# Sums of exponentials in four column tiles throughout, and the last sums one round later

## The chip, the cores and the metric

The kernel runs on one core of a Trainium2 chip. A core has five engines that work side by side, each from its own queue in order: TensorE (PE; matrix products into PSUM, with the weight loads counted apart as PEld), VectorE (DVE), ScalarE (ACT), GpSimd (POOL) and SyncE (SP, which here issues nearly all DMA transfers). The metric is the device time of one execution in microseconds, the median over several runs; lower is better. A profiled execution gives a trace, and from it a page and the answers of views.

## The reference

Attention over 4 batches and 8 heads, 768 positions, 64 dimensions each. Queries and keys are assigned to one of 16 clusters by the largest cosine with that head's centroids, and a query sees only keys of its own cluster. Then a feed-forward block (FFN) with a squared ReLU over all 3072 rows.

```
mask = q_assign[:, :, :, None] == k_assign[:, :, None, :]
scores = scale * np.matmul(q, k.transpose(0, 1, 3, 2))
scores = np.where(mask, scores, -1000000000.0)
...
attn = np.exp(scores)
attn = attn / (np.sum(attn, axis=-1, keepdims=True) + 1e-09)
x = np.matmul(attn, v)      # (B,H,S,D) -> (B*S, H*D)
r = np.maximum(x @ w_in, 0.0)     # 512 -> 2048
out = (r * r) @ w_out             # 2048 -> 512
```

The diff touches `np.sum(attn)` and the division by it.

## The kernel before

**Tiling.** Heads go in pairs: pair 0 to 15, four to a batch, the two heads of a pair (`e` = 0, 1) on 64 partitions each. A pair has two halves `h` of 384 queries (`TB`), and a half takes six chunks of 128 keys, two to a step. The steps are the list `units` (line 725), 96 of them: first the first halves of pairs 0 to 3 (units 0 to 11), then their second halves (12 to 23), then pairs 4 to 15 with both halves each (24 to 95).

**One unit.** `scores` (line 439) multiplies queries and keys on TensorE and takes the exponential on ScalarE. For pairs 0 to 3 the mask goes into the same products, for the others VectorE applies it (line 470). `times_v` (line 502) multiplies the exponentials with v into the PSUM tile `av`, 64 rows for each head.

**The sums.** They are products with a constant block `ups`, so each row of the result holds the same sum. For the first halves of pairs 0 to 3 they are taken from the exponentials by 8 products for each unit, in the tile `sm` of the same pool as `av` (`ps_av`, two buffers). For all other halves GpSimd adds the exponentials of a half up in `acc` (lines 480 and 482), and `add_up` (line 529) forms the sums from `acc` with four products when the half is complete. Each fp32 product is two matmul instructions in the trace.

`ones_products` (line 486) has two forms. The usual one splits the 384 queries into two groups, so that two heads by two groups fill four column tiles of 32 rows, each over 192 columns. The `wide` form, for pair 3's first half alone (line 498), uses two column tiles of 64 rows, each over all 384 columns, so that every row of `av` finds its sum on its own partition.

**The division.** In the usual form `add_up` takes the reciprocal `r` of 192 columns (line 551), writes one row of each tile to memory (`far_r`, line 554), reads it back spread over 64 partitions for each head (`rb`, line 558), and puts a copy in `seen` (line 555), which is checked at the end for sums that are too small (`check_sums`, line 866). In between, `seen` is issued ahead of `rb` on SP. In a first half `av` is copied to `xT` by ScalarE before (line 536). One round later `finish` (line 567) multiplies by `rb`. In the wide form the reciprocal of 384 columns goes straight to `rb` (line 545), and `finish` follows in the same round, from `av`.

**The order.** The main loop (line 791) runs a round for each unit: its scores; `ends(added)`, the `finish` of halves that `add_up` has handled in the round before; the `times_v` of earlier units (one round behind, and from unit 12 on in twos, in the odd rounds); `add_up` of completed halves (for second halves of pairs 0 to 3 one round later, through the list `late`); rounding of the FFN's weights on ScalarE, VectorE and GpSimd (line 141; lines 150 to 166; up to round 23); and `fill_steps`.

`fill_steps` (line 746) issues plain FFN products of batch 0 between the attention's work (the generator `ffn`, line 579: for each half 64 products `ph` of 384 columns and 48 products `po` of 512). The share of a round is worked out from the columns left, less a reserve of three `po` products; from round 13 on it is given in even rounds only, for two at a time. A half's FFN becomes available when `finish` of pair 3 has been issued for it: for the first half in round 12. After the loop the rest is issued, and then batches 1 to 3 go through `ffn_pair` (line 610), seven block products in place of eight, with eight PSUM banks, till the end.

This is the order of the source; the framework's planner works out each engine's queue from it, by priority (`high_priority` raises it) among the instructions that its own estimate holds to be ready, and sets the waits.

Of the kernel before, what the change touches and what calls it, by code (L numbers as in the profile page):

```python
# [8 lines left out]
F32 = mybir.dt.float32  # L9
# [9 lines left out]
P = 128  # L19
# [6 lines left out]
def kernel(  # L26
# [10 lines left out]
    nc = tc.nc  # L37

    B, H, S, D = q.shape
    C = centroids.shape[1]  # L40
    NCH = S // P
# [4 lines left out]
    HP = H // 2  # L46
    NB = NCH // 2
    TB = NB * P
# [382 lines left out]
    sums = {}  # L431
# [4 lines left out]
    av = {}  # L436
# [46 lines left out]
                out=acc[pair, h], in0=acc[pair, h], in1=t[:, 2 * i : 2 * i + 2], op=ALU.add  # L483
            )

    def ones_products(sm, wide, e, rhs, first, last):

        n = TB if wide else TB // 2
        rows = P * n // (2 * TB)
        return [  # L490
            dict(
                out=sm[rows * r : rows * (r + 1)], lhsT=ups[:, 0:rows],
                rhs=rhs[:, n * i : n * (i + 1)], start=first, stop=last,
            )
            for i, r in enumerate(range(e * P // (2 * rows), (e + 1) * P // (2 * rows)))
        ]

    def wide(pair, h):

        return (pair, h) == (HP - 1, 0)  # L500

    def times_v(pair, h, c):
        if c == 0:
            av[pair, h] = ps_av.tile([P, TB], F32, name="av", tag="av")
            if first_half(pair, h):
                n = TB if wide(pair, h) else TB // 2
                sums[pair, h] = ps_av.tile([P, n], F32, name="sm", tag="av")
        t = ex.pop((pair, h, c))
        products = [
            dict(  # L510
                out=av[pair, h][D * e : D * (e + 1)], lhsT=raw_v[pair][:, e, c + i],
                rhs=t[:, 2 * i + e], start=(c + i == 0), stop=(c + i == NCH - 1),
            )
            for i in range(2) for e in range(2)
        ]
        if first_half(pair, h):
            for i in range(2):
                one = [
                    ones_products(
                        sums[pair, h], wide(pair, h), e, t[:, 2 * i + e], c + i == 0, c + i == NCH - 1  # L520
                    )
                    for e in range(2)
                ]
                products += [p for both in zip(*one) for p in both]
        together(products, 4000)
# [3 lines left out]
    def add_up(pair, h):  # L529


        b, hp = divmod(pair, HP)
        if first_half(pair, h):
            sm = sums.pop((pair, h))
            if not wide(pair, h):
                nc.scalar.copy(out=xT_of(b, h)[:, hp], in_=av.pop((pair, h)))
        else:
            total = acc.pop((pair, h))
            sm = bank("sm", [P, TB // 2])
            one = [ones_products(sm, False, e, total[:, e], True, True) for e in range(2)]  # L540
            together([p for both in zip(*one) for p in both])
        row = 4 * (2 * pair + h)
        if wide(pair, h):
            rb = rbp.tile([P, TB], F32, name="rb")
            nc.vector.reciprocal(out=rb, in_=sm)
            nc.sync.dma_start(
                seen[row : row + 4], rb.rearrange("(e p) (g n) -> e p g n", e=2, g=2)[:, 0]
            )
        else:
            r = once.tile([P, TB // 2], F32, name="r")  # L550
            nc.vector.reciprocal(out=r, in_=sm)  # L551
            r = r.rearrange("(r p) n -> r p n", r=4)[:, 0]
            far = dram.tile([2, TB], F32, name="far_r")
            nc.sync.dma_start(far.rearrange("e (g n) -> (e g) n", g=2), r)
            nc.sync.dma_start(seen[row : row + 4], r)
            rb = rbp.tile([P, TB], F32, name="rb")
            for e in range(2):
                nc.sync.dma_start(rb[D * e : D * (e + 1)], far[e].partition_broadcast(D))
        spread_out[pair, h] = rb

    def xT_of(b, h):
# [222 lines left out]
    def ends(halves):  # L784
        for pair, h in halves:
            b, hp = divmod(pair, HP)
            finish(pair, h)
            if hp == HP - 1 and (b, h) in PLAIN:
                fill.append(ffn(b, h))

    for u in range(len(units) + 2):
        if u < len(units):
            pair, h, c = units[u]
            if (p := next_pair(u)) is not None:
# [18 lines left out]
        while v_next < min(ready, len(units)):  # L813
            pair, h, c = units[v_next]
            times_v(pair, h, c)
            v_next += 1
            if c == NCH - 2:
                (late if u < HP * NCH and h else complete).append((pair, h))
        for pair, h in complete:
            with tc.high_priority(offset=1000) if first_half(pair, h) else ExitStack():  # L820
                add_up(pair, h)
            if h == 1:
                for d in (qkT, ids, qid):
                    d.pop(pair)
            if h == 1 or pair < HP:
                raw_v.pop(pair)
            if wide(pair, h):
                with tc.high_priority(offset=1000):
                    ends([(pair, h)])
            else:  # L830
                added.append((pair, h))

        rounding += 4
        while rounding >= 3:
# [263 lines left out]
```

## Time and profile before

| | |
|---|---|
| median of 3 runs | 984.49 us (984.35 to 984.61) |
| profiled run, and its span in the trace | 984.76 us, 983.0 us |
| rounds 0 to 95 with the plain FFN of batch 0 | to 542.6 us |
| `ffn_pair` of batches 1, 2 and 3 | 542.6 to the end, some 145 us each |
| pair 3's first half: its sums, reciprocal, `finish` | start at 70.77, 77.10, 81.59 us |
| last half (pair 15, h = 1): sums, reciprocal, `finish` | start at 534.57, 535.50, 545.04 us |

How to read the lines that follow. In the page's first part each engine has its busy time, share of the span and number of instructions. A line of waits says which engine waited with which tile and source line, for whom, and then the total in us, the number of times and the longest. A line of the timeline has the start and duration in us, engine, source line, operation, output and inputs, shape, and the count if several are put together; in brackets stands how long the engine was idle before it, and who ended that. Line 91 is the first product of a group that `together` (line 88) issues, line 94 the others. A line of windows has the stretch, its length, the busy time of PE, PEld, DVE, ACT and POOL with instruction counts, the granted TensorE clock (1.00 is full), the DMA engines' busy share, and GB/s.

### The profile page before, as it was taken

The page shows a single profiled execution, that of the slowest core. Times are in us where ns is not written, and L with a number is a line of the kernel's source. Part 1 is how long each engine was busy: PE and PEld are TensorE (multiplying, and loading weights), DVE is VectorE, ACT ScalarE, POOL GpSimd, SP SyncE. Part 2 cuts the span into 40 slices and gives each one's busy share as a digit, 9 for nine tenths or more (in the row PEclk, how much of TensorE's full clock was granted, in tenths as well). Part 3 has the DMA queues.
Part 4 walks back from the last instruction along what each step waited for, and adds up shares of the span by engine and source line. Part 5 has one row for each costly group of instructions (what it writes and reads, how often), then busy time and mean ns, then how long its engine had stood idle before and what let it go on. Part 6 is the DMA issues. An engine that isn't in the chain of part 4 may idle for free.

```text
span 983.0 us, 12011 instructions
## 1 busy us (share of the span) xinstructions
PE 962.6 (98%) x4455; PEld 552.8 (56%) x4455; DVE 562.4 (57%) x913; ACT 315.4 (32%) x510; POOL 376.9 (38%) x277
## 2 busy tenths in 40 slices
PE   7999989999999999999999999999999999999997
PEld 4544444443344444443343555888556888556886
DVE  5777778766566665667654865532566531656331
ACT  5886755444445545544231111000111000111000
POOL 1336666655656556565666231002231002231000
PEclk9999999999999999999999999999999999999999
DMA  9666572534546345452310000000000000000000
GB/s 248 199 186 177 164 212 76 136 108 106 135 111 156 98 109 123 111 142 75 74 42 16 15 0 1 11 22 22 11 1 1 21 22 22 1 0 1 22 22 24
DMA packets 127575, 74.32 MB, mean 76 GB/s; under 512 B 90906, under 2 KB 118934, under 8 KB 127510
## 3 DMA queue, kind: packets, MB, share of 16 engines
q1 hardware_dynamic: 125798, 73.06, 28.1%
q8 instruction: 37, 0.61, 0.3%
q10 hardware_dynamic: 1712, 0.43, 0.2%
q14 instruction: 28, 0.23, 0.1%
HBM read 48.07 MB, written 15.86 MB: 65 GB/s over the span
## 4 chain that ended last, share of the span: by engine, by line
PE 81%; DVE 6%; DMA 5%; issue 3%; ACT 1%; POOL 1%; SPq 1%; ACTq 0%; DVEq 0%; POOLq 0%
PE bank L707 22%; PE bank L676 22%; PE po L597 7%; PE ph L584 6%; PE sc L91 6%; PE sc L94 5%; PE av L91 5%; PE av L94 4%; DMA rb<-far_r 3%; DVE w_raw L162 1%; DVE r L551 1%; PE sm L91 1%; DVE ex L470 1%; DMA far_r<-r 1%; POOL w_in L166 1%
## 5 line engine op out<-in xcount | busy, mean ns | idle before, releaser
L482 POOL TENSOR_TENSOR acc<-acc,ex 128x768 f32<-128x768 f32 x112 | 207.1, 1849 | 115.0 <-DVE ex L470 98.4
L470 DVE SCALAR_TENSOR_TENSOR ex<-qid,ids,sc 128x384 f32<-128x384 bf16 x288 | 157.7, 608 | 63.3 <-ACT sc L466 45.6
L466 ACT ACTIVATE sc<-sc 128x768 f32<-128x768 f32 x144 | 108.5, 792 | 162.1 <-PE sc L94 144.6
L94 PE MATMUL sc<-qkT 64*128 64x384 f32 x576 | 153.4, 505 | 0.7
L94 PE MATMUL av<-ex,v_raw 128*64 128x384 f32 x576 | 136.9, 495 | 0.0
L665 POOL TENSOR_TENSOR w_s<-w_in 128x256 f32<-128x256 f32 x24 | 18.3, 762 | 279.9 <-PE bank L707 162.0
L646 DVE TENSOR_TENSOR g<-bank,g 128x384 f32<-128x384 f32 x144 | 77.9, 556 | 81.5 <-PE bank L676 80.5
L707 PE MATMUL bank<-w_out,g 128*128 128x256 f32 x432 | 95.2, 379 | 0.0
L584 PE MATMUL ph<-xT,w_in 128*128 128x384 f32 x256 | 91.8, 498 | 3.3 <-DVE best L341 2.3
L597 PE MATMUL po<-w_out,gT 128*128 128x512 f32 x192 | 92.7, 615 | 0.0
L91 PE MATMUL sc<-qkT 64*128 64x384 f32 x192 | 87.9, 538 | 2.6 <-DVE ex L470 2.6
L707 PEld LDWEIGHTS bank<-w_out,g 128*128 128x128 f32 x432 | 82.1, 190 | 11.8
L646 DVE TENSOR_TENSOR osb<-bank,osb 128x256 f32<-128x256 f32 x54 | 22.1, 423 | 107.6 <-PE bank L707 102.2
L94 PEld LDWEIGHTS sc<-qkT 64*128 64x128 f32 x576 | 65.4, 187 | 28.6 <-issue 6.7
L91 PE MATMUL av<-ex,v_raw 128*64 128x384 f32 x192 | 81.0, 504 | 0.0
L676 PE MATMUL bank<-xT,w_in 128*128 128x384 f32 x192 | 69.9, 487 | 0.0
L676 PE MATMUL bank<-x_t,w_s 128*128 128x384 f32 x192 | 69.8, 486 | 0.0
L676 PE MATMUL bank<-xT,w_s 128*128 128x384 f32 x192 | 69.8, 486 | 0.0
L584 PEld LDWEIGHTS ph<-xT,w_in 128*128 128x128 f32 x256 | 45.6, 189 | 42.7 <-issue 16.0
L94 PEld LDWEIGHTS av<-ex,v_raw 128*64 128x64 f32 x576 | 49.8, 137 | 34.6 <-issue 34.4
L480 POOL TENSOR_TENSOR acc<-ex 128x768 f32<-128x768 f32 x28 | 51.0, 1822 | 46.9 <-DVE ex L470 39.0
L707 PE MATMUL bank<-w_t,g_s 128*128 128x256 f32 x288 | 65.1, 379 | 0.0
(128 smaller groups left out, 1222.8 us busy)
## 6 DMA issues: line engine op xcount, KB each, us to landing
words<-flat SPq DMA_DIRECT2D x24, 384.0 KB
w_raw<-in_moe_w_in_dram SPq DMA_DIRECT2D x16, 512.0 KB
w_raw<-in_moe_w_out_dram SPq DMA_DIRECT2D x16, 512.0 KB
v_raw<-in_v_dram SPq DMA_DIRECT2D x20, 384.0 KB
q_raw<-in_q_dram SPq DMA_DIRECT2D x31, 192.0 KB
k_raw<-in_k_dram SPq DMA_DIRECT2D x31, 192.0 KB
rb<-far_r SPq DMA_DIRECT2D x62, 96.0 KB
out_dram<-osb SPq DMA_DIRECT2D x23, 256.0 KB
```

Source lines behind the costliest of these rows:

```text
L91: last = nc.tensor.matmul(**next(products))
L94: last = nc.tensor.matmul(**product)
L466: last_exp[0] = nc.scalar.activation(out=t[:, 2 * i : 2 * i + 2] if pair < HP else src, in_=src, func=ACT.Exp, scale=SCALE).ins
L470: nc.vector.scalar_tensor_tensor(out=t[:, 2 * i + e], in0=qid[pair][1][:, h, e], scalar=ids[pair][:, ch % NB, 2 + ch // NB, e : e + 1], in ...
L480: nc.gpsimd.tensor_tensor(out=acc[pair, h], in0=t[:, 0:2], in1=t[:, 2:4], op=ALU.add)
L482: nc.gpsimd.tensor_tensor(out=acc[pair, h], in0=acc[pair, h], in1=t[:, 2 * i : 2 * i + 2], op=ALU.add)
L584: nc.tensor.matmul(ph, lhsT=w_in[:, kk, f * P : (f + 1) * P], rhs=xT[b, h][:, kk], start=(kk == 0), stop=(kk == KT - 1),)
L597: nc.tensor.matmul(po, lhsT=gT[f][:, i * P : (i + 1) * P], rhs=w_out[:, f], start=(f == 0), stop=(f == FT - 1),)
L646: nc.vector.tensor_tensor(out=out, in0=bank, in1=to, op=ALU.add)
L665: nc.gpsimd.tensor_tensor(out=s1, in0=a[1][0], in1=a[1][1], op=ALU.add)
L676: nc.tensor.matmul(bank, lhsT=operands[j][0][:, kk], rhs=operands[j][1][:, kk], start=(kk == 0), stop=(kk == H2 - 1),)
L707: nc.tensor.matmul(bank, lhsT=operands[j][0][:, f], rhs=operands[j][1][:, f], start=(f == 0), stop=(f == F2 - 1),)
```

## The change

The wide form goes. `ones_products` has one form, four column tiles of 32 rows, and so pair 3's first half takes the way of the others: a copy of `av` to `xT` on ScalarE, a reciprocal of 192 columns, through memory to `rb`, and `finish` in the next round (with a raised priority). Its FFN half becomes available in round 13, and as shares are given in even rounds, the first plain products come in round 14. In every `add_up`, `seen` is issued behind the two `rb` transfers. Second halves that complete in the rounds after the last unit also go through `late`, so pair 15's last sums come in round 97 and its `finish` in round 98, and the loop has one round more; what the shares are worked out from (`ENDS`) stays.

By the arithmetic of the shares, the plain products in round 12, then in 14, 16, 18, 20, 22 and 24, number 5, 11, 11, 10, 10, 10, 5 before and 0, 11, 11, 11, 11, 11, 6 after; round 96 and round 97 have two each and three stay for the end, before and after.

```diff
@@ -483,28 +483,22 @@
                 out=acc[pair, h], in0=acc[pair, h], in1=t[:, 2 * i : 2 * i + 2], op=ALU.add
             )
 
-    def ones_products(sm, wide, e, rhs, first, last):
-
-        n = TB if wide else TB // 2
-        rows = P * n // (2 * TB)
+    def ones_products(sm, e, rhs, first, last):
+
+        n, rows = TB // 2, P // 4
         return [
             dict(
-                out=sm[rows * r : rows * (r + 1)], lhsT=ups[:, 0:rows],
-                rhs=rhs[:, n * i : n * (i + 1)], start=first, stop=last,
-            )
-            for i, r in enumerate(range(e * P // (2 * rows), (e + 1) * P // (2 * rows)))
+                out=sm[rows * (2 * e + g) : rows * (2 * e + g + 1)], lhsT=ups[:, 0:rows],
+                rhs=rhs[:, n * g : n * (g + 1)], start=first, stop=last,
+            )
+            for g in range(2)
         ]
-
-    def wide(pair, h):
-
-        return (pair, h) == (HP - 1, 0)
 
     def times_v(pair, h, c):
         if c == 0:
             av[pair, h] = ps_av.tile([P, TB], F32, name="av", tag="av")
             if first_half(pair, h):
-                n = TB if wide(pair, h) else TB // 2
-                sums[pair, h] = ps_av.tile([P, n], F32, name="sm", tag="av")
+                sums[pair, h] = ps_av.tile([P, TB // 2], F32, name="sm", tag="av")
         t = ex.pop((pair, h, c))
         products = [
             dict(
@@ -517,7 +511,7 @@
             for i in range(2):
                 one = [
                     ones_products(
-                        sums[pair, h], wide(pair, h), e, t[:, 2 * i + e], c + i == 0, c + i == NCH - 1
+                        sums[pair, h], e, t[:, 2 * i + e], c + i == 0, c + i == NCH - 1
                     )
                     for e in range(2)
                 ]
@@ -532,30 +526,22 @@
         b, hp = divmod(pair, HP)
         if first_half(pair, h):
             sm = sums.pop((pair, h))
-            if not wide(pair, h):
-                nc.scalar.copy(out=xT_of(b, h)[:, hp], in_=av.pop((pair, h)))
+            nc.scalar.copy(out=xT_of(b, h)[:, hp], in_=av.pop((pair, h)))
         else:
             total = acc.pop((pair, h))
             sm = bank("sm", [P, TB // 2])
-            one = [ones_products(sm, False, e, total[:, e], True, True) for e in range(2)]
+            one = [ones_products(sm, e, total[:, e], True, True) for e in range(2)]
             together([p for both in zip(*one) for p in both])
         row = 4 * (2 * pair + h)
-        if wide(pair, h):
-            rb = rbp.tile([P, TB], F32, name="rb")
-            nc.vector.reciprocal(out=rb, in_=sm)
-            nc.sync.dma_start(
-                seen[row : row + 4], rb.rearrange("(e p) (g n) -> e p g n", e=2, g=2)[:, 0]
-            )
-        else:
-            r = once.tile([P, TB // 2], F32, name="r")
-            nc.vector.reciprocal(out=r, in_=sm)
-            r = r.rearrange("(r p) n -> r p n", r=4)[:, 0]
-            far = dram.tile([2, TB], F32, name="far_r")
-            nc.sync.dma_start(far.rearrange("e (g n) -> (e g) n", g=2), r)
-            nc.sync.dma_start(seen[row : row + 4], r)
-            rb = rbp.tile([P, TB], F32, name="rb")
-            for e in range(2):
-                nc.sync.dma_start(rb[D * e : D * (e + 1)], far[e].partition_broadcast(D))
+        r = once.tile([P, TB // 2], F32, name="r")
+        nc.vector.reciprocal(out=r, in_=sm)
+        r = r.rearrange("(r p) n -> r p n", r=4)[:, 0]
+        far = dram.tile([2, TB], F32, name="far_r")
+        nc.sync.dma_start(far.rearrange("e (g n) -> (e g) n", g=2), r)
+        rb = rbp.tile([P, TB], F32, name="rb")
+        for e in range(2):
+            nc.sync.dma_start(rb[D * e : D * (e + 1)], far[e].partition_broadcast(D))
+        nc.sync.dma_start(seen[row : row + 4], r)
         spread_out[pair, h] = rb
 
     def xT_of(b, h):
@@ -784,11 +770,13 @@
     def ends(halves):
         for pair, h in halves:
             b, hp = divmod(pair, HP)
-            finish(pair, h)
+
+            with tc.high_priority(offset=1000) if (pair, h) == (HP - 1, 0) else ExitStack():
+                finish(pair, h)
             if hp == HP - 1 and (b, h) in PLAIN:
                 fill.append(ffn(b, h))
 
-    for u in range(len(units) + 2):
+    for u in range(len(units) + 3):
         if u < len(units):
             pair, h, c = units[u]
             if (p := next_pair(u)) is not None:
@@ -815,7 +803,7 @@
             times_v(pair, h, c)
             v_next += 1
             if c == NCH - 2:
-                (late if u < HP * NCH and h else complete).append((pair, h))
+                (late if h and not HP * NCH <= u < len(units) else complete).append((pair, h))
         for pair, h in complete:
             with tc.high_priority(offset=1000) if first_half(pair, h) else ExitStack():
                 add_up(pair, h)
@@ -824,11 +812,7 @@
                     d.pop(pair)
             if h == 1 or pair < HP:
                 raw_v.pop(pair)
-            if wide(pair, h):
-                with tc.high_priority(offset=1000):
-                    ends([(pair, h)])
-            else:
-                added.append((pair, h))
+            added.append((pair, h))
 
         rounding += 4
         while rounding >= 3:
```

## The prediction

> **What bounds the kernel now.** I read the page's first part, the waits of TensorE alone, the timelines at the two places that the diff touches, and the busy time and granted clock in short windows.
>
> ```profile
> PE 962.6 (98%) x4455; PEld 552.8 (56%) x4455; DVE 562.4 (57%) x913; ACT 315.4 (32%) x510; POOL 376.9 (38%) x277
> ```
>
> TensorE is the bound almost everywhere, so a product less, or a wait less in its queue, comes off the span unless something else takes its place. Its own waits are few:
>
> ```profile
> PE sc L91 <- DVE ex L470: 2.6, 3, 1.1
> PE sm L91 <- POOL acc L482: 2.3, 1, 2.3
> PE ph L584 <- DVE best L341: 2.3, 1, 2.3
> ...
> PE ph L584 <- DVE xT L570: 0.8, 1, 0.8
> ```
>
> The second is the wait of pair 15's second half (the last one) for its sums; the fourth is the first plain FFN's wait for pair 3's first half. Both stand where the diff works. The tail's timeline:
>
> ```profile
> 530.82 3.69 POOL L482 TENSOR_TENSOR acc<-acc,ex 128x768 f32<-128x768 f32 x2 [1.54 <-DVE ex L470]
> 534.57 0.53 PE L91 MATMUL sm<-acc,ups 128*32 128x192 f32 x1 [2.33 <-POOL acc L482]
> 535.36 7.43 PE L597 MATMUL po<-w_out,gT 128*128 128x512 f32 x14
> 542.63 1.45 PE L676 MATMUL bank<-xT,w_in 128*128 128x384 f32 x4
> ```
>
> and its windows (span, then busy time of PE, PEld, DVE, ACT, POOL, then the granted clock):
>
> ```profile
> 532.00:534.00 2.00, 0.24 (x2) 0.00 (x0) 0.00 (x0) 0.00 (x0) 1.92 (x2) 1.00 0.00 0
> 534.00:536.00 2.00, 1.43 (x9) 0.70 (x10) 0.50 (x1) 0.00 (x0) 2.00 (x4) 0.58 0.00 0
> 536.00:538.00 2.00, 2.00 (x4) 0.76 (x3) 0.86 (x1) 0.00 (x0) 2.00 (x4) 0.57 0.01 4
> 538.00:540.00 2.00, 2.00 (x6) 0.86 (x5) 0.45 (x2) 0.00 (x0) 2.00 (x3) 1.00 0.05 15
> ```
>
> TensorE stands still for 2.33 us, and then runs some 3.4 us at 0.57 of its clock: the wait is paid twice. TensorE at the other place:
>
> ```profile
> 58.23 2.16 PE L94 MATMUL sm<-ex,ups 128*32 128x192 f32 x48
> 60.32 0.84 PE L382 MATMUL po<-ident_b,oh 128*128 128x128 bf16 x12
> ...
> 70.77 4.04 PE L94 MATMUL sm<-ex,ups 128*64 128x384 f32 x24
> 74.73 0.59 PE L91 MATMUL sc<-qkT 64*128 64x384 f32 x1
> ...
> 79.28 2.20 PE L584 MATMUL ph<-xT,w_in 128*128 128x384 f32 x6
> 82.29 1.53 PE L584 MATMUL ph<-xT,w_in 128*128 128x384 f32 x4 [0.81 <-DVE xT L570]
> ```
>
> The same sums take 2.09 us in four column tiles (58.23 to 60.32) and 3.96 us in two (70.77 to 74.73). VectorE there:
>
> ```profile
> 62.84 1.34 DVE L551 RECIPROCAL r<-sm 128x192 f32<-128x192 f32 x1
> 70.92 0.56 DVE L570 SCALAR_TENSOR_TENSOR xT<-xT,rb 128x384 f32<-128x384 f32 x1 [2.05 <-DMA rb<-far_r]
> 77.10 2.54 DVE L545 RECIPROCAL rb<-sm 128x384 f32<-128x384 f32 x1
> 81.59 0.55 DVE L570 SCALAR_TENSOR_TENSOR xT<-av,rb 128x384 f32<-128x384 f32 x1
> ```
>
> Pair 2's way through memory takes 6.7 us from the reciprocal's end (64.18) to the scaling, pair 3's direct way 1.95 us (79.64 to 81.59, other VectorE work between).
>
> **What the Trainium skill says.** "TensorE: Matmul & The Clock Gate", Part 1, says that an idle window of about 3.4 us takes the array to half its clock and a busy one gives it back, the windows running free. The trace agrees in kind: 0.57 for 3.4 us, here after 2.33 us of idleness. The same page, Part 3, says that products in different column tiles run at once, about 4 ns apart; the trace agrees (48 in 2.09 us, or 174 ns for four of 326 ns). It also says that VectorE's and ScalarE's queues are strictly in order, so one waiting instruction holds all behind it; the 2.05 us above is such a wait. "DMA: Bandwidth & Descriptors", "Anatomy of one DMA", puts a transfer's fixed cost at about 2 us, mostly its receipt; that is for another issue path, but the trace has 1.6 us for far_r when memory is quiet and 2.1 to 2.6 us for it under the weight loads.
>
> **The change, part by part.**
>
> Sums of pair 3, first half. 24 instructions of 384 columns in pairs become 48 of 192 in fours: 3.96 - 2.09 = 1.87 us of TensorE less, on the path.
>
> The last sums. From the end of the last av (531.55 + 0.69 = 532.24) to the first bank product (542.63) TensorE takes 10.39 us. At full clock the work is one set of sums (0.47 us, as from 520.87 to 521.34) and seven po products, 14 instructions 0.43 us apart as around 513: 6.02. The 3.9 us beyond these 6.49 are the wait and its slow clock. By the share arithmetic two products come between av and sums in round 96, two in round 97, three last; the title says five ahead of the sums. Five (10 x 0.43 + 0.15 = 4.45 us) cover the wait wholly; two (1.87 us) leave 0.46 us of it, too short, I judge, for the clock to fall. Gain 3.4 to 3.9; I take 3.9.
>
> Given back there: behind five products the sums start at 536.7, the reciprocal at 537.6 (0.93 later, as now), far_r at 539.0, rb's issue at 540.7 (1.66 later, as now), and rb is in 3.57 us after that (524.46 to 528.03): 544.2. The scaling ends at 544.8. The FFN pair now starts at 538.7 and its 5th product at 543.9 (1.29 apart, as from 542.63 to 543.92); ScalarE's first copy to g already waits 2.33 us for that scaling. Which PSUM bank is av's isn't shown: if the 5th product's, it waits 0.9 us; later in line, nothing; if VectorE's w_t (2.29 each) goes ahead of the scaling, up to 2.5. I take 0.9. Tail: -3.0.
>
> Five plain products leave round 12. They take 79.28 to 83.75 now, 4.47 us for 10 x 0.32 = 3.2 of work: 1.27 us of waiting goes. Since round 13 is odd, the fill starts at round 14; 3.2 us of work is spread over later rounds, no gain or loss. Does TensorE starve in rounds 12 and 13? Scores of round 12 start 1.87 earlier at 72.86, round 13's at 77.41, round 14's at 80.66, its fill at 82.48 (steps of 4.55, 3.25, 1.82 as in the trace). ScalarE has from 70.8 to 82.5 two exponentials (1.51 each), flat (1.58), about four roundings (1.38 each) and the added copy (0.48): 10.6 of 11.7 us. It holds, narrowly, so nothing is charged.
>
> The way through memory. Its scaling must be there for the fill's fourth product at 82.48 + 6 x 0.32 = 84.4. The shorter reciprocal (1.35 for 2.54) waits for roundings ahead of it in VectorE's queue; I take its end at 77.3 (between 76.5 and 78.5). The three first-half pairs before need 7.7, 6.4 and 6.7 us from there to the scaling, the second half of pair 0 needs 10.8. So it ends at 84.3 to 85.6, at worst 88.7: a wait of 0 to 4.3, I take 0.6. VectorE, which now idles 5.46 us until 87.61 for ScalarE, idles for rb instead; behind it are roundings, after them SP's weight loads, nearer only to TensorE at `best` (wait of 2.28 before 130.73). VectorE is busy 21.57 of 26 us from 84 to 110, so it can't come forward as far as TensorE does: that wait grows by 0 to 1.5, I take 0.6. First half: -1.87 - 1.27 + 0.6 + 0.6 = -1.9.
>
> The seen transfer behind rb. rb's issue waits for far_r, which lands 1.6 us or more after its issue; seen's 0.55 us on SP fits in that now. So rb comes no sooner (0 to 0.3 us from emptier rings), and what follows on SP comes 0.55 us later, 31 times; loads run ahead by more. Taken as nothing. The last seen lands later, near 544, and VectorE's check of seen (0.44) may stand ahead of w_t: inside the 2.5 us above.
>
> Sum: -3.0 - 1.9 = -4.9 us against the profiled span of 983.0; the profiled run took 984.76, the median is 984.49, so the difference is applied to that: **979.6**.
>
> **The rivals.** *Only the tail pays.* The new wait before the fourth product or the longer one at `best` eats the first half's gain: 984.5 - 3.0 = 981.5. For it: VectorE's load until 130; against: 1.87 us of work that is simply gone.
> *Only the first half pays.* The planner leaves the sums ahead of most plain products, or the late scaling holds a bank and VectorE's adds: tail -0.5, so 984.5 - 1.9 - 0.5 = 982.1.
> *Everything pays.* No new wait and the `best` wait (2.28 us and then a clock of 0.63, another 1.7 us or so) falls away by the shift: -3.9 - 1.9 - 1.3 - about 2 of that: 975.5.
> *Slower.* Place: pair 3's rb on SP. Its issue stands behind weight loads that wait for POOL, POOL for VectorE's rounding; one such turn cost 4.7 us at 106.97 to 111.70. With two turns and the transfer, 17 us after 77.3, the scaling ends near 94.9, VectorE resumes 7.3 us later than its 87.61, and `best` and TensorE move with it: +7.3 - 3.0 is +4.3, so 988.8. It decides from a scaling later than about 92.6 (87.6 + 3.0 + 2.0) for a loss of 0.2%. Against it: 10.8 us is the longest seen.
>
> **How the numbers follow.** Likeliest 0.42, only the tail 0.22, only the first half 0.08, everything 0.16, slower 0.12. Measurements of this kernel tell about 0.2%, 2.0 us, from no change: 982.5 to 986.5 is the same. Of the second and third case 0.03 each falls there; so faster 0.82, same 0.06, slower 0.12. The range leaves out the slower case and a small part of the first four: 975.3 to 983.6.
>
> **What would show it.** Right: 48 sm instructions in 2.1 us for pair 3; no PE wait for acc at the end and a clock of 1.00 from 530 to 543; the FFN pair's first product about 5 us sooner; a PE wait for xT under 1.5 us near 84. Wrong: a PE wait for bank near 545, a `best` wait above 4 us, or rb more than 11 us behind pair 3's reciprocal.

## The result, and the profile after

The changed kernel takes 980.5 us (median of six runs, 976.7 to 981.6) against 984.55 us for the kernel before (six runs, 983.5 to 984.8): a ratio of 0.9955, 95% interval 0.9939 to 0.9971. The forecast was 979.6. The span of the profiled execution went from 983.0 to 978.4 us.

The first part of the page of the changed kernel:

```profile
PE 958.9 (98%) x4479; PEld 552.0 (56%) x4479; DVE 562.2 (57%) x913; ACT 315.4 (32%) x511; POOL 375.9 (38%) x277
```

24 TensorE instructions more (48 in place of 24 in pair 3's sums) and one ScalarE instruction more (the copy), as the change says. TensorE's own waits in the changed kernel, the four that matter here:

```profile
PE sc L91 <- DVE ex L470: 3.8, 4, 2.5
PE ph L570 <- DVE xT L556: 2.8, 1, 2.8
...
PE ph L570 <- DVE best L341: 0.8, 1, 0.8
PE sm L91 <- POOL acc L482: 0.4, 1, 0.4
```

The last wait for `acc` fell from 2.3 to 0.4 us, that for `best` from 2.3 to 0.8. Two waits grew: that of the first plain FFN for `xT` (0.8 to 2.8), and the longest wait of a scores product for the masks (1.1 to 2.5), which the forecast doesn't mention. The tail in the timeline of the changed kernel:

```profile
529.37 3.69 POOL L482 TENSOR_TENSOR acc<-acc,ex 128x768 f32<-128x768 f32 x2 [1.67 <-DVE ex L470]
530.72 1.98 PE L583 MATMUL po<-w_out,gT 128*128 128x512 f32 x4
533.11 0.35 PE L91 MATMUL sm<-acc,ups 128*32 128x192 f32 x1 [0.41 <-POOL acc L482]
...
533.58 4.56 PE L583 MATMUL po<-w_out,gT 128*128 128x512 f32 x10
537.97 1.45 PE L662 MATMUL bank<-xT,w_in 128*128 128x384 f32 x4
```

Two products (four instructions) stand between the last `av` and the sums, five behind them. So five is the number behind the sums, not ahead of them as the forecast took it. TensorE at the first half:

```profile
69.93 2.16 PE L94 MATMUL sm<-ex,ups 128*32 128x192 f32 x48
72.01 0.59 PE L91 MATMUL sc<-qkT 64*128 64x384 f32 x1
...
81.63 2.20 PE L570 MATMUL ph<-xT,w_in 128*128 128x384 f32 x6
86.63 7.09 PE L570 MATMUL ph<-xT,w_in 128*128 128x384 f32 x16 [2.80 <-DVE xT L556]
```

The sums take 2.08 us (69.93 to 72.01) where they took 3.96. The fill's fourth product waits 2.80 us for pair 3's scaling, and the 16 instructions behind it take 7.09 us, where 16 x 0.32 = 5.1 would be full speed. VectorE there:

```profile
75.41 1.35 DVE L537 RECIPROCAL r<-sm 128x192 f32<-128x192 f32 x1
...
84.35 2.13 DVE L556 SCALAR_TENSOR_TENSOR xT<-xT,rb 128x384 f32<-128x384 f32 x1 [3.33 <-DMA rb<-far_r]
```

The windows of the changed kernel (length, busy PE, PEld, DVE, ACT, POOL, then the granted clock):

```profile
84.00:88.00 4.00, 1.37 (x4) 0.93 (x5) 3.62 (x5) 2.56 (x5) 2.03 (x3) 0.97 0.84 244
88.00:92.00 4.00, 4.00 (x9) 2.10 (x8) 3.96 (x4) 0.74 (x3) 3.92 (x3) 0.60 0.38 78
...
466.00:470.00 4.00, 3.73 (x10) 1.45 (x11) 2.43 (x6) 1.59 (x2) 2.61 (x2) 0.58 0.31 70
...
530.00:534.00 4.00, 3.59 (x18) 1.25 (x15) 0.29 (x1) 0.00 (x0) 3.92 (x4) 1.00 0.00 0
534.00:538.00 4.00, 4.00 (x11) 1.74 (x10) 1.77 (x3) 0.00 (x0) 4.00 (x7) 1.00 0.02 5
```

In the tail the clock stays at 1.00 through the short wait. After the two longer waits (near 84 and near 466) it falls to about 0.6 for one window. These are means over windows that hold part of a dip: from 87.77 to 91.16 us the granted clock is 0.50, and so it is in the kernel before from 534.32 to 537.72, where the forecast reads 0.57.

**Where the time went.** I cut each trace at the starts of the scores of units 11, 25, 83, 85 and 95 and at the first block product of `ffn_pair`. In us, by stretch:

| stretch | before | after | difference |
|---|---|---|---|
| start of unit 11 | 67.61 | 66.67 | -0.94 |
| units 11 to 25 (first half, `best`) | 99.40 | 96.53 | -2.87 |
| units 25 to 83 | 297.72 | 296.30 | -1.42 |
| units 83 to 85 (a late wait) | 10.69 | 13.58 | +2.89 |
| units 85 to 95 | 51.04 | 51.81 | +0.77 |
| 95 to the first block product (tail) | 16.17 | 13.08 | -3.09 |
| the rest | 440.37 | 440.43 | +0.06 |

The sum is -4.6 us. The first row is not of the change: the code up to there is the same, and in 13 profiled executions with that code unit 11 starts anywhere between 66.65 and 68.06. It goes with the speed of TensorE in the first 20 us. In three of them, the kernel before among them, the granted clock is 0.64 to 0.68 from 16 to 20 us, and unit 11 starts at 67.46 to 67.61; in three more the first product of `lg` (queries or keys with the centroids), at some 9 us, takes 0.85 us in place of 0.51, and unit 11 starts at 67.96 to 68.06; in the other seven, with neither, at 66.65 to 66.82. Units 25 to 83 scatter too (296.30 and 297.53 in two executions of the changed kernel). The late wait and the +0.77 had to be explained, and whether the 2.80 us wait is a loss.

### The profile page after: what moved, and what is told of

Read it like the earlier page. It is cut to its first block, busy times and chain, and to the rows that moved or that the text cites. A ratio compares the mean times of both kernels' runs of the same rounds, so it can differ in the third digit from the quotient of the medians.

```text
span 978.4 us, 12070 instructions
## 1 busy us (share of the span) xinstructions
PE 958.9 (98%) x4479; PEld 552.0 (56%) x4479; DVE 562.2 (57%) x913; ACT 315.4 (32%) x511; POOL 375.9 (38%) x277
## 4 chain that ended last, share of the span: by engine, by line
PE 50%; DVE 0%; DMA 0%; POOL 0%; issue 0%; SPq 0%; DVEq 0%; POOLq 0%
PE bank L693 22%; PE bank L662 22%; PE po L583 3%; PE sc L91 1%; PE sc L94 1%; PE av L91 1%; PE av L94 1%; POOL acc L482 0%; DMA rb<-far_r 0%; DVE ex L470 0%; PE sm L91 0%; DMA far_r<-r 0%; DVE r L537 0%; PE lg L91 0%; SPq L543 0%
## 5 line engine op out<-in xcount | busy, mean ns | idle before, releaser
L693 PE MATMUL bank<-w_t,g 128*128 128x256 f32 x288 | 65.1, 379 | 0.0
```

The lines of the kernel that those rows point to most:

```text
L693: nc.tensor.matmul(bank, lhsT=operands[j][0][:, f], rhs=operands[j][1][:, f], start=(f == 0), stop=(f == F2 - 1),)
```

## The experiments

My theory: the tail is worth 3 us by a wait that goes, and the first half about 2 us less what the wait for `xT` gives back. Rivals: the late wait is the change's doing; a product order without the `xT` wait would gain that time; or VectorE bounds the stage from there up to pair 4's route (`best`), so that whatever TensorE gains there is waited away. In the quoted expectations, a time is the median or its difference as it says. "The subtractions" are VectorE's four preparations of batch 1's `ffn_pair` (line 604 of the changed kernel), issued during the late rounds.

### The two parts alone, and the change again

The tail alone, made on the kernel before; all else stays:

```diff
-    for u in range(len(units) + 2):
+    for u in range(len(units) + 3):
...
-                (late if u < HP * NCH and h else complete).append((pair, h))
+                (late if h and not HP * NCH <= u < len(units) else complete).append((pair, h))
```

> The kernel before with the tail's part alone (two plain products between the last av and the last sums; every other queue's order is that of before). If the profiled difference of the tail is its worth (10.39 us before, 7.19 us after, from the last av to the first product of the FFN pair): 3.2 us less than before, some 981.3 us, the clock 1.00 in the tail. Rival, that the tail is worth the wait alone and the half clock comes back elsewhere: 1.9 us less, 982.6. Rival, that the tail is worth nothing by itself since the late scaling then holds the FFN pair: 984.5.

Measured: 981.79 us, ratio to before 0.9968 (0.9957 to 0.9980), so -3.2 us. The tail stretch takes 12.85 us in place of 16.17. This kernel has the order of the kernel before up to unit 95, and yet its late wait is there, in TensorE's waits of the tail-alone kernel:

```profile
PE sc L91 <- DVE ex L470: 3.8, 3, 2.5
```

Units 83 to 85 take 13.76 us. So the late wait isn't of the change; the one profiled execution of the kernel before was spared it, and so were two with the changed first half (10.69 us in each). The pair of profiles thus understates the change by 2.9 us there.

The changed kernel without the tail part (the two lines above, back):

> The kernel after without the tail's part (the last sums in front of all seven products again). If the first half's part is nearly cancelled within itself, as the two traces suggest (sums -1.9, the first fill's wait and its half clock +3.2, the wait at best -3.1, the late wait for VectorE's mask +2.9, small shifts -1 to -2): 0 to 1.5 us less than before, 983 to 984.5 us. Rival, the prediction's working (first half worth 1.9 or more): 982.6 or less. Rival, first half worth 3.1 (sums and the old wait in round 12): 981.4.

Measured: 983.02 us, ratio 0.9988 (0.9973 to 1.0002), so -1.2 us with an interval from -2.7 to +0.2: less than my 1.9, though not told apart from it. Its last sums stand where they stood before and wait 2.33 us for `acc`, as before, but here no slow clock follows (1.00 from 534 to 538), and the tail takes 14.57 us instead of 16.17. So about half of the 3.3 us in the tail is the slow clock, which one execution pays and another doesn't; the last section shows what it goes with.

The changed kernel again, beside other runs of the kernel before:

> The kernel after, unchanged, beside the variants on one chip. If what was measured holds: 0.995 to 0.997 of the kernel before, 979.7 to 981.5 us. The late wait of scores for ex (2.48 us at 466 in the first profile of after, 0.87 in that of before, 2.5 in the run with the tail alone, whose order up to there is that of before) tells the executions apart, not the kernels: in this profile it is anything from 0.5 to 2.5 us.

Measured: 981.28 us, ratio 0.9956 (0.9938 to 0.9974). Its wait for `xT` is 2.55 us, its late wait 2.5, `best` 0.9: the picture holds. Tail alone and first half alone add up to -4.4 us; both together gave -4.4 and -4.3 (ratios 0.9955 and 0.9956).

### What the wait for `xT` costs

Six of the profiled executions have the order of the changed kernel up to unit 25. Three of them have the long wait for `xT`: 2.80 and 2.55 us (the changed kernel twice) and 3.33 (five products, below). The other three have a short one: 1.04 us (first half alone), 0.78 and 1.08 (subtractions moved, without and with five products, below). Yet units 11 to 25 take 96.53, 97.34 and 98.13 us with the long wait, and 96.56, 96.30 and 98.26 with the short. Where it is short, TensorE waits later, as these lines of the waits with the subtractions moved show:

```profile
PE ph L570 <- DVE best L341: 1.8, 1, 1.8
...
PE ph L570 <- DVE r L537: 1.3, 1, 1.3
...
PE ph L570 <- DVE xT L556: 0.8, 1, 0.8
```

Which of the two comes goes with who is first, the scaling or the second of GpSimd's two adds. The same execution:

```profile
85.20 0.56 DVE L556 SCALAR_TENSOR_TENSOR xT<-xT,rb 128x384 f32<-128x384 f32 x1 [3.11 <-ACT ex L466]
83.42 4.03 POOL L482 TENSOR_TENSOR acc<-acc,ex 128x768 f32<-128x768 f32 x2
```

In the three executions with the short wait the scaling starts 0.12 to 0.60 us ahead of the second add (here 85.20, 85.32) and takes 0.56 to 0.94 us; in the three with the long one it starts 0.07 to 0.19 us behind it and takes 2.05 to 2.16 us.

Keep the roundings of rounds 11 and 12 back, so that VectorE is free for pair 3:

```diff
-        while rounding >= 3:
+        while rounding >= 3 and u not in (11, 12):
```

> The kernel after, with no weight rounded in rounds 11 and 12 (made up for in round 13). If the new wait of 2.80 us for pair 3's scaling comes from its reciprocal standing behind roundings on VectorE (sums done at 72.0, reciprocal at 75.4): the reciprocal moves up by some 2 to 3 us, the wait and its half clock fall to under 0.5 us, and the total falls by 2 to 4.5 us, to 976 to 978.5. Rival, that the way through memory alone fills the time and a wait over 2 us stays: no change, 980.5. Rival, that the roundings made up for come in the way of the route of pair 4 (wait at best of 0.75 us in after): what is gained is lost there, 980 to 983.

Measured: 983.1 us, ratio 0.9992 (0.9979 to 1.0005). The wait for `xT` fell to 0.51 us, but TensorE's waits of this kernel now begin with this line,

```profile
PE ph L570 <- ACT gT L577: 5.1, 1, 5.1
```

and the timeline of ScalarE in it shows what the wait is for:

```profile
90.70 0.67 ACT L150 ACTIVATE w_out<-w_raw 128x512 f32<-128x512 f32 x1 [3.32 <-DMA w_raw<-in_moe_w_out_dram]
...
94.33 0.85 ACT L577 ACTIVATE gT<-ph 128x384 f32<-128x384 f32 x2
```

The roundings kept back are made up in later rounds and stand in ScalarE's queue ahead of the copies that free the banks of the plain products; they wait for weight loads, which come later too. Units 11 to 25 take 101.08 us. The wait moved to another engine, and grew.

Finish pair 3 in its own round again, through memory, so the plain products stay in round 12:

```diff
-            added.append((pair, h))
+            if (pair, h) == (HP - 1, 0):
+                ends([(pair, h)])
+            else:
+                added.append((pair, h))
```

> The kernel after, with pair 3's scaling issued in round 12, so that the plain products stay in rounds 12 and 13 as in before (four, then one) and meet the way through memory there. If the later start of the fill is what hides the way through memory: the fourth product waits from about 78 until the scaling at 84 to 86, some 6 us with a half clock after it, and the total is 2 to 5 us above after, 982.5 to 985.5 us. Rival, that VectorE and the rounding bound this stage and TensorE catches up anyway: within 1 us of after, 980 to 981.5.

Measured: 986.76 us, ratio 1.0016 (0.9999 to 1.0032); against the changed kernel on the same chip (0.9956) that is 0.0060 x 985, or 5.9 us, more than expected. TensorE's waits in this kernel:

```profile
PE ph L570 <- DVE xT L556: 3.9, 1, 3.9
...
PE ph L570 <- DVE r L537: 2.2, 1, 2.2
PE ph L570 <- DVE best L341: 1.9, 1, 1.9
```

From 80 to 88 us VectorE works 1.82 us, since it waits 3.35 us for `rb` ahead of pair 3's scaling and then 2.89 us for ScalarE's part of the rounding; from 84 to 88 the granted clock is 0.60. Units 11 to 25 take 103.74 us here, against 96.53 and 97.34. What makes the way through memory bearable is that the fill starts two rounds later.

Now take the wait away and leave all else: of the first eight plain products (two `ph` groups of four), the six that need pairs 0 to 2 go first, the two that need pair 3 last.

```diff
+        gT, ph, order_f = [], {}, [(f, kk) for f in range(FT) for kk in range(KT)]
+        if (b, h) == (0, 0):
+            order_f[0 : 2 * KT] = sorted(order_f[0 : 2 * KT], key=lambda p: p[1] == KT - 1)
+        for f, kk in order_f:
+            ph[f] = bank("ph", [P, TB]) if kk == 0 else ph[f]
...
```

> The kernel after, with the order of the first eight plain products changed alone: the six that need pairs 0 to 2 first, then the two that need pair 3. Three more products (1.9 us) stand ahead of the wait for pair 3's scaling. If that wait of 2.80 us and its half clock (1.7 us) cost what they seem to: the wait falls to about 0.9 us, the clock stays up, and the total falls by 1.9 to 3.6 us, 977 to 978.8 us. Rival, that the stage is bound by VectorE up to the route of pair 4 (its wait for best grows by what is gained): no change, 980.5.

Measured: 980.61 us, ratio 0.9955 (0.9938 to 0.9973): what the changed kernel has (0.9956). The waits are in its timeline:

```profile
87.11 3.67 PE L571 MATMUL ph<-xT,w_in 128*128 128x384 f32 x10 [0.55 <-DVE xT L556]
...
101.69 6.72 PE L571 MATMUL ph<-xT,w_in 128*128 128x384 f32 x20 [1.43 <-DVE r L537]
...
125.94 0.88 PE L571 MATMUL ph<-xT,w_in 128*128 128x384 f32 x2 [1.76 <-DVE best L341]
```

The wait for `xT` is 0.55 us and the clock stays at 1.00. Counted from unit 11, TensorE is 3.7 us ahead of the changed kernel at unit 15, 1.2 at unit 20, and 0.15 at unit 25: two later waits for VectorE took it back (against the second profile of the changed kernel it is 0.96 ahead at unit 25). From unit 11 to 15 it takes 23.25 us, and the three executions with a short wait and the old order take 23.27 to 23.57; so this one profile can't tell the new order from such an execution, but the measured times show no gain from it. The 2.80 us wait is large and yet costs nearly nothing.

That VectorE bounds the stage was then tried by taking work off it: the kernel just shown without the clamp of the rounded weights (weights outside the clamp's range stay as they are), one of VectorE's three passes for each weight tile.

```diff
-        nc.vector.tensor_scalar(
-            out=dst.bitcast(F32), in0=dst.bitcast(F32), scalar1=2.0 ** -15, scalar2=HIGHEST,
-            op0=ALU.max, op1=ALU.min,
-        )
```

> The kernel with the six plain products first (whose gain of 3.7 us at unit 15 was given back by unit 25), leaving out the clamp of the weights between 2^-15 and the highest value (one VectorE pass of 0.4 to 2 us for each of 32 weight blocks). If VectorE bounds the stage up to the route of pair 4: TensorE's waits for best and r in that stage (1.8 and 1.4 us) fall to under 0.5 us, unit 25 comes 2 to 5 us sooner after unit 11 than the 96.4 us of that kernel, and the total falls by as much, to 976 to 978.5. Rival, that the stage is bound by ScalarE's copies or by transfers: unit 25 moves by less than 1 us, 980 to 980.6.

Measured: 974.66 us, ratio 0.9897 (0.9864 to 0.9930). Units 11 to 25 take 91.66 us instead of 96.38, and no TensorE wait at all is left between 84 and 135 us. The gain is larger than expected, over six runs. This stage hangs on VectorE's passes, then, and not on the order of the products. Whether by VectorE's own time, or by what waits for these passes on ScalarE and GpSimd, which share the rounding, this run doesn't separate.

### More products ahead of the last sums

The changed kernel with what I had assumed, five products in round 96 (`DM` is the columns of one):

```diff
+        share = share if u < len(units) else 5 * DM * (u == len(units))
```

> The kernel after, with all five plain products that aren't kept for the end in round 96, ahead of the last sums (after has two there). The wait of 0.4 us for acc goes. If the prediction's working of the tail holds: rb lands 2.2 us later than in after, about 5 us after the FFN pair's first product, the scaling holds ScalarE's first copy or a bank, and 0.5 to 2.5 us are lost: 981 to 983. Rival, that eight banks are slack enough: 0.4 us less than after or no change, 980 to 981.

Measured: 980.16 us, ratio 0.9955 (0.9937 to 0.9972), as with two. TensorE in the timeline of this kernel:

```profile
532.88 4.56 PE L583 MATMUL po<-w_out,gT 128*128 128x512 f32 x10
537.36 0.35 PE L91 MATMUL sm<-acc,ups 128*32 128x192 f32 x1
...
547.71 1.53 PE L662 MATMUL bank<-xT,w_s 128*128 128x384 f32 x4 [0.16 <-DVE xT L556]
```

and VectorE in it:

```profile
539.85 5.04 DVE L604 TENSOR_TENSOR w_t<-w_out 128x2048 f32<-128x2048 f32 x2 [0.53 <-PE po L583]
544.82 2.28 DVE L604 TENSOR_TENSOR w_t<-w_out,w_t 128x2048 f32<-128x2048 f32 x1
547.02 0.55 DVE L556 SCALAR_TENSOR_TENSOR xT<-av,rb 128x384 f32<-128x384 f32 x1
```

The wait for `acc` is gone and the tail 0.5 to 0.7 us shorter (12.36); but three `w_t` now run on VectorE ahead of the scaling, which ends at 547.57, and the seventh block product waits for it. The rest takes 440.75 us, 0.3 to 0.5 more than in the two executions of the changed kernel. What five would add in front is given back behind for the most part.

### The late wait

VectorE's lines in the changed kernel, ahead of the late wait:

```profile
460.01 2.56 DVE L604 TENSOR_TENSOR xT<-xT 128x768 f32<-128x768 f32 x1
462.50 0.55 DVE L556 SCALAR_TENSOR_TENSOR xT<-av,rb 128x384 f32<-128x384 f32 x1
462.97 2.10 DVE L604 TENSOR_TENSOR x_t<-x_t,xT 128x768 f32<-128x768 f32 x1
464.99 2.18 DVE L470 SCALAR_TENSOR_TENSOR ex<-qid,ids,sc 128x384 f32<-128x384 bf16 x4
```

GpSimd beside them in the timeline of the changed kernel:

```profile
459.37 4.88 POOL L482 TENSOR_TENSOR acc<-acc,ex 128x768 f32<-128x768 f32 x2 [3.13 <-DVE ex L470]
```

and both engines in the timeline of the kernel before:

```profile
464.62 5.75 POOL L482 TENSOR_TENSOR acc<-acc,ex 128x768 f32<-128x768 f32 x2 [3.14 <-DVE ex L470]
465.26 0.95 DVE L618 TENSOR_TENSOR xT<-xT 128x768 f32<-128x768 f32 x1
...
467.02 1.68 DVE L618 TENSOR_TENSOR x_t<-x_t,xT 128x768 f32<-128x768 f32 x1
```

A subtraction of 0.95 us takes 2.56 and 2.10 us beside GpSimd's adds, and the masks behind it reach TensorE 2.5 us late. The scaling between the two, which reads `av` from PSUM, takes 0.55 us beside the same adds. In the profile of before the third subtraction (465.26) came through in 0.95 us, and GpSimd's two adds took 5.75 us instead of 3.6 or 3.7.

In both profiles the first add starts the same time behind the second subtraction (459.37 behind 459.15, 464.62 behind 464.39). They part where that subtraction ends: in one the add goes next, in the other the third subtraction. Ten executions have the subtractions in this place. In seven units 83 to 85 take 13.50 to 13.94 us; in three (the kernel before, the roundings kept back, the clamp left out) they take 10.69, and GpSimd's two adds 5.75 or 5.76.

So the four subtractions were put behind the last unit's masks on VectorE. In the changed kernel:

```diff
...
-                nc.vector.scalar_tensor_tensor(
+                last_mask[0] = nc.vector.scalar_tensor_tensor(
...
-                )
+                ).ins
...
-        with tc.issue_after(last_exp[0]):
+        with tc.issue_after(last_mask[0]):
```

> The kernel after, with the four subtractions that prepare batch 1's FFN pair put behind the last unit's masks on VectorE (they stood at 456 to 465 us; nothing else moves in any queue). If TensorE's wait of 2.48 us at 466 us and the half clock after it (about 1.7 us) come from these subtractions standing ahead of a mask: 3 to 4 us less than after, 976.5 to 977.5 us, and no wait of scores for ex over 1 us there. Rival, that the stall comes from GpSimd's adds or from rb at that place: no change, 980.5. Rival, that the subtractions at the end hold the FFN pair's second product: 1 to 3 us gained at 466 and lost at 540, 979.5 to 980.5.

Measured: 978.52 us, ratio 0.9944 (0.9930 to 0.9958). Units 83 to 85 take 9.34 us, the late wait is gone. At the end GpSimd's last adds now meet the first subtraction, which starts just before them (both engines in the timeline of this kernel):

```profile
526.15 0.95 DVE L604 TENSOR_TENSOR x_t<-xT 128x768 f32<-128x768 f32 x1
526.38 4.86 POOL L482 TENSOR_TENSOR acc<-acc,ex 128x768 f32<-128x768 f32 x2 [1.43 <-DVE ex L470]
```

The two adds take 4.86 us instead of 3.69, TensorE waits 1.6 us for them, and the tail takes 14.02 us, 0.9 to 1.2 more. Net, 1 us or so better than the changed kernel by the ratios, where 3 to 4 were expected; their intervals overlap.

The same move in the kernel before:

> The kernel before with the four subtractions behind the last masks. If the late wait for the mask is no consequence of the change but of these subtractions in both kernels (2.5 us in the trace with the tail alone, 0.9 in the one of before): 2 to 3 us less than before, 981 to 982.5. Rival, that the change moved VectorE into that wait: no change to before, 984 to 985.

Measured: 983.56 us, ratio 0.9986 (0.9972 to 1.0000). Units 83 to 85 take 9.35 us here too, and the wait for `acc` at the end, 2.33 us before, grows to 3.50. The tail takes 18.80 us, 2.6 more than in the kernel before. So the subtractions make the late wait in both kernels, and the move pays more where products stand ahead of the last sums.

The subtractions moved and the products reordered, in the changed kernel:

> Both edits: the six products first, and batch 1's four subtractions behind the last masks. If the two waits are independent, their gains add up: 2.0 (from the subtractions, 978.5 for 980.5) and 1.9 to 3.6, so 975 to 976.6 us. Rival, VectorE binds the stage before: 978.5.

Measured: 978.87 us, ratio 0.9932 (0.9908 to 0.9957). The reordering adds nothing that could be told apart here either.

The subtractions moved and five products ahead of the sums:

> The kernel after with the four subtractions behind the last masks, and five products ahead of the last sums. With the subtractions alone TensorE waited 1.6 us for acc at the end (they slow GpSimd's last adds); five products cover that. If nothing else moves: 1 to 1.6 us less than with the subtractions alone (978.5), 977 to 977.5. Rival, the late scaling holds the FFN pair: 978.5 to 980.5.

Measured: 978.43 us, ratio 0.9940 (0.9922 to 0.9957). The wait for `acc` is gone and the tail down to 12.36 us, but the seventh block product waits 1.25 us, here for GpSimd's `w_s` (line 604), and the rest takes 441.73 us, 1.3 more than in the changed kernel. Again the gain in front is given back behind. The three changed kernels with the subtractions moved (978.4 to 978.9 us) have the lowest times of the kernels that leave nothing out. They are ahead of the kernel before; none of them is told apart from the changed kernel, nor from one another.

## Why the prediction was right, and which steps were not

As a whole, -4.9 us was forecast; the ratio gives -4.4 (-6.0 to -2.9).

**Sums in four tiles: right.** 1.87 us forecast; 3.96 - 2.08 = 1.88 measured.

**The tail: right in size, with a wrong number in it.** Forecast -3.0, made up of 3.9 gained and 0.9 given back. Measured -3.1 and -3.3 in the two executions of the changed kernel, -3.3 and -3.2 us by trace and by ratio with the tail alone. But I took five products as standing ahead of the sums, against my own arithmetic of shares. The trace has two, with a wait of 0.41 us (0.46 worked out for two) and a clock that holds, as I had judged for that case. And nothing is given back with two: the scaling starts at 540.71, and no block product waits. With five, as it was run, the give-back is 0.16 us of wait, and 0.3 to 0.5 in the rest of the span, not 0.9: three `w_t` (5.04 and 2.28 us) do stand ahead of the scaling, but it is the seventh block product that waits for it, two later than I had taken. That the sum came out at -3.0 is luck in part: a gain taken too high by some 0.7 us and a loss of 0.9 that isn't there nearly cancel.

**The wait for pair 3's scaling: mis-sized.** I had 0.6 us with a range of 0 to 4.3. The changed kernel's two profiles have 2.80 and 2.55 and a slow clock in the next window on top; of the four other executions with its order, one has 3.33 and three 0.78 to 1.08. The way through memory is not where it went wrong. Counted from unit 11, since this execution was 0.94 us ahead there, TensorE reached the fill as reckoned (14.96 us, I had 14.87), the reciprocal ended 0.4 us later (10.09 for 9.69), and the scaling started 7.6 us behind it, within the 6.4 to 7.7 that I had. The larger part of the excess of 2.2 us, 1.6 us, is the scaling itself: it took 2.13 us instead of the 0.56 I took from pair 2's, and GpSimd's two adds run from 82.35 to 86.07. The Trainium skill, "SBUF — State Buffer", "SBUF: two separate sides", says that VectorE (when both inputs are in SBUF) and GpSimd share a pair of ports, and that the one that starts first keeps it for its whole instruction. The durations agree here: the scaling ends 0.41 us after the adds do, and in the late wait the subtraction from 462.97 ends at 465.07, 0.82 us after GpSimd's adds at 464.25; the scaling there with one input in PSUM isn't slowed (0.55). Who starts first doesn't decide everywhere: in the kernel before the add of 464.62 started ahead of the third subtraction (465.26), and the subtraction went first. No run changed the ports alone, so this cause is read from the durations, not tried.

**`best`: wrong sign, right reason.** I had it grow by 0.6 us; it shrank from 2.28 to 0.75. With the long wait at the scaling and the slow clock behind it, TensorE arrived at `best` later than I had reckoned. In the three executions with the short wait, `r` and `best` together hold it 3.1 us, 0.8 more than `best` before; there my 0.6 comes near. The reason I gave, that VectorE can't come forward as far as TensorE does, is what the reordered products and the missing clamp showed: take 3.7 us of wait away at unit 15, and 0.15 is left at unit 25; take a VectorE pass away, and 4.7 us come off the stretch. My two terms of +0.6 were one pot that VectorE fills: what isn't waited at the scaling is waited at `r` and `best`. The three waits add up to 3.4 to 4.2 us in all six executions.

**Ten instructions out of round 12 with "no gain or loss": one product was overlooked.** By the shares, 62 plain products went out up to round 24 before and 61 do now. One `ph` (0.64 us) less is in units 11 to 25, and the work shows again at the end of the fill: units 85 to 95 take 51.80 us in every kernel with the later fill, and 50.94 to 51.04 in the four with the fill in round 12 (before, tail alone, round 12 again, subtractions moved in before). That is 0.8 to 0.9 us, as much as one `po` (2 x 0.43). Over six executions with the changed first half and its product order, units 11 to 25 average 97.19 us (96.30 to 98.26), over three with that of before 98.69 (98.16 to 99.40): -1.5. Units 25 to 83 average 296.61 us in the six (296.13 to 297.53) and 297.81 in the three (297.72 to 297.88): -1.2, of which the moved products (one `ph` more, one `po` less) explain 0.2; the rest stays open. With the +0.8 that makes some -1.9 us, which is what I forecast, but 1.2 of it in a stretch where I had forecast nothing: luck as a sum. By the measured times the first half is worth -1.2 (-2.7 to +0.2).

**`seen` behind `rb`: nothing, for another reason.** SyncE's queue in the changed kernel:

```profile
76.78 0.52 SPq L540 DMA_DIRECT2D far_r<-r  x1
77.36 0.53 SPq L544 DMA_DIRECT2D seen<-r  x1
...
79.97 1.14 SPq L543 DMA_DIRECT2D rb<-far_r  x2
```

`seen` is still issued between the two, here and for all 32 halves in this trace; the planner puts what is ready first. The edit moved a line of the source and nothing in the queue. Hence no run for it alone.

**The rivals.** "Only the tail pays" (981.5) comes nearest among them: the tail is three quarters of the gain. "Everything pays" is out: it needed no new wait and none at `best`, and the waits for VectorE in this stage still add up to 3.4 us or more. "Slower" would have needed a scaling later than 92.6; it ended at 86.48.

Of the signs I had named, the sums in 2.1 us and the clock at 1.00 came true; the FFN pair started 4.66 us sooner (about 5, though 0.94 of it is the start of this execution and 2.9 went to the late wait); the last `acc` wait isn't zero but 0.41; the wait for `xT` missed its bound of 1.5 us in the changed kernel's two profiles and kept it in three other executions.

## What to carry to other kernels

A wait of the bound engine that ends a stage with nothing behind it pays in full when other work is put ahead of it, and just enough work is enough: more of it delays what hangs on the waiting instruction. A wait in the middle of a stage that another engine bounds is only where the time happens to be seen; find out by taking the wait away (the reordered products) and by taking work off the suspected engine (the missing clamp) before it is worth mending. Compare two kernels over several executions and by stretch, for one pair of profiles here mixed 0.9 us of start and 2.9 us of a late wait into a gain of 4.6, and showed a wait of 2.80 us that was 0.78 in another execution of the same order.

## What was not expected of the hardware

- The length of a wait alone doesn't decide what it does to the granted clock. In a trace the clock changes at times that lie a whole number of 3.413 us apart (changed kernel: 87.76, 91.17, 466.64, 470.05). Each of the 14 traces can be cut at such times (here between 20 and 960 us). All 15 stretches in which TensorE stood still for 1.95 us or more were followed by a clock of 0.50; of the 38 with 0.9 to 1.85 us, two were (1.59 and 1.78). So it matters where a wait falls. The wait of 2.33 us for `acc` in the kernel before lay with 2.07 us in one stretch:

```profile
530.91:534.31 3.40, 1.33 (x8) 0.53 (x5) 0.00 (x0) 0.00 (x0) 3.32 (x2) 1.00 0.00 0
534.32:537.72 3.40, 3.15 (x11) 1.38 (x12) 1.36 (x1) 0.00 (x0) 3.40 (x6) 0.50 0.01 2
```

  With the first half alone the same wait was split over two, and the clock stayed:

```profile
529.83:533.23 3.40, 2.23 (x14) 0.95 (x10) 0.67 (x2) 0.00 (x0) 2.51 (x2) 1.00 0.00 0
533.24:536.64 3.40, 2.25 (x12) 1.02 (x13) 1.36 (x1) 0.00 (x0) 3.40 (x5) 1.00 0.00 0
536.65:540.05 3.40, 3.40 (x9) 1.52 (x8) 0.76 (x2) 0.00 (x0) 3.26 (x5) 1.00 0.12 36
```

  The Trainium skill, "TensorE: Matmul & The Clock Gate", Part 1, has an idle window of about 3.4 us for this; here some 2 us within one such stretch were enough.
- VectorE's operations with both inputs in SBUF went from 0.56 to 2.13 us and from 0.95 to 2.56 us beside GpSimd's adds; where VectorE went first, GpSimd's two adds took 5.75 us instead of some 3.7.
- Which of the two engines goes first at the late wait differs between executions that arrive there in the same order, 0.22 or 0.23 us apart. What decides it stays open, and with it why the one profiled execution of the kernel before was spared.
